# Retention and two MoE layers on one core: the next block's x split behind the second tile's transposes, one mean subtraction on VectorE, S1's parts ahead of two copies

## The chip, the core and the metric

The kernel runs on one core of a Trainium2 chip. The core has TensorE (matmuls and transposes, PE in the rows), VectorE (DVE), ScalarE (ACT), GpSimd (POOL) and SyncE (SP, which here issues most DMA transfers). Each engine runs its own queue in order; semaphores tie the queues together. The metric is the device time of one execution in microseconds (us), less is better. The time of a kernel is the median over its runs.

## The reference

Retention over 768 positions (4 sequences, 8 heads of 64), then a gated layer and then a second layer with a softmax-like unit and a layer norm, on 3072 tokens of 512. Everything is float32:

```python
state = gamma[None, :, None, None] * state + np.einsum('bhd,bhe->bhde', k[:, :, t], v[:, :, t])
y[:, :, t] = scale * np.einsum('bhd,bhde->bhe', q[:, :, t], state)
...
xn = x / rms * rms_g
silu = g * (1.0 / (1.0 + np.exp(-g)))          # g = xn @ w_gate, val = xn @ w_val
x2 = silu * val @ w_out                        # d_ff 1536
...
h = x2 @ w_in                                  # 1024 wide
sm = e / (np.sum(e, axis=-1, keepdims=True) + 1e-09)   # e = exp(h - max)
solu = h * sm
ln = (solu - mu) / np.sqrt(var + 1e-06) * g_ln
return (ln @ w_out).astype(np.float32)
```

## The kernel before

**Blocks.** The tokens are worked in six blocks of 512 (n = 0 to 5), and each block has two stages. The first (gate, value and out, in 12 chunks) makes x2 in the four banks X0 to X3 of PSUM (`XB`). The second, the D stage, makes h, its unit and the result in tiles t = 0 to 3 of 128 tokens. While block n runs, retention for a later block, its x (`xT`) and the next block's first products are worked in the gaps of the same queues. Every product of two float32 matrices is three matmuls on fp32r values: each operand is split in a high part and a low part, and the products high x high, high x low and low x high are summed. `split` (lines 99 to 102) makes the two parts of a tile: a cast on ScalarE gives the high part (line 100), and a subtraction gives the low part (line 101) on VectorE or, where it says so, on GpSimd.

**The D stage of blocks 2 to 5** is `de_quarters` (line 1090). It forms h with seven products of quarters instead of eight (`p1` to `p7`; matmuls on line 1141), whose operands include sums S1 to S4 of quarters of x2. S1 is split on VectorE, S3 and S4 on GpSimd, S2 inline (lines 1116 and 1117). `keep` copies a bank with ScalarE (line 1151) and `add` adds a bank to what is kept with VectorE (line 1155). Then four steps are made for each tile, in this order: soft(2), soft(0), t_tr(2), soft(3), soft(1), t_tr(0), e_mm(2), t_tr(3), e_mm(0), t_tr(1), e_mm(3), e_mm(1). Tile 2 is therefore the first and tile 0 the second.

- `soft` (line 983) computes exp, the products h x e with their sums (line 997), the mean (lines 999 and 1000) and subtracts the mean (line 1002): the first half of 512 columns on VectorE, the second on GpSimd.
- `t_tr` (line 1007) transposes the tile, four transposes of 128 columns for each of two banks (line 1013), casts each bank to its high part (line 1016, ScalarE) and takes the low part (line 1017, VectorE). A square (line 1020) and small operations (lines 1022 to 1028) give the factor of the layer norm.
- `e_mm` (line 1031) is the last product, 24 matmuls (lines 771 to 773), the scaling of its bank (line 1053) and the store (line 1054).

**The next x.** In blocks 2 and 3 the x of the next block is split in four pieces by `xn_split_t`, low parts on GpSimd. Block 5 is the one whose gate and value products use the seven-product form too (`SEVEN`), so block 4 runs `x_sums` (line 425) instead: three splits of plain pieces, four differences (line 437) and four splits of sums into tiles tagged rq, rk, kd and qd. All low parts and differences are GpSimd's. Their matmuls are those of line 883.

**What sets the order.** The program is written as steps hung on numbered slots: `extra[(n, s)]` holds what is emitted when the slot s of block n comes. The slots of the next x stand in the tuple `r` of the block loop. A scheduler then orders the instructions of each engine when the program is built. `tc.issue_after(i)` is a constraint on that order: what is issued under it is placed behind i. It is no semaphore and no wait on the chip. `recent["hi"]` names the instruction behind which the splits of the next x are placed.

Of the kernel before, what the change touches and what calls it, by code (L numbers as in the profile page):

```python
# [9 lines left out]
F32 = mybir.dt.float32  # L10
# [5 lines left out]
ALU = mybir.AluOpType  # L16
# [26 lines left out]
def retention_moe_kernel(ctx: ExitStack, tc: tile.TileContext, qk0, q2, kt, kv, wpk, w2i, w2o,  # L43
# [936 lines left out]
    def halves(t):  # L980
        return t[:, 0, :], t[:, 1, :]

    def soft(n, t, H, e, u, final):
        V = nc.vector
        sm = wt("sm", [P, 12], F32, 4)
        mx, se, su = sm[:, 0:2], sm[:, 2:4], sm[:, 4:6]
        nmx, mu = sm[:, 6:7], sm[:, 7:8]
        for hf in range(2):
            V.tensor_reduce(out=mx[:, hf:hf + 1], in_=H[hf], axis=AX.X, op=ALU.max)
        V.tensor_reduce(out=nmx, in_=mx, axis=AX.X, op=ALU.max, negate=True)  # L990
        for hf in range(2):
            nc.scalar.activation(e[hf], H[hf], AF.Exp, bias=nmx, accum_out=se[:, hf:hf + 1])
        if final and n not in (1, NB - 1) and PRE & 1:

            nc.scalar.activation(sm[:, 11:12], se[:, 1:2], AF.Silu)
        for hf in range(2):
            V.scalar_tensor_tensor(out=u[:, hf, :], in0=H[hf], scalar=1.0, in1=e[hf],
                                   op0=ALU.mult, op1=ALU.mult, accum_out=su[:, hf:hf + 1])
        V.tensor_tensor(out=mu, in0=su[:, 0:1], in1=su[:, 1:2], op=ALU.add)
        V.tensor_scalar(mu, mu, 1.0 / D_FF2, None, ALU.mult)  # L1000
        for hf, eng in ((0, V), (1, nc.gpsimd)):
            i = eng.tensor_scalar(u[:, hf, :], u[:, hf, :], mu, None, ALU.subtract)
            if eng is V:
                recent["sub"] = i
        lnst[t] = (u, sm)

    def t_tr(t, banks=None):
# [3 lines left out]
        for b in range(2):  # L1011
            bank = (banks or HB[t])[b]
            recent["t"] = run([lambda j=j: nc.tensor.transpose(bank[:, j * P:j * P + P], u[:, b, j * P:j * P + P], ident)  # L1013
                 for j in range(4)])
            hi, lo = r2(), r2()
            nc.scalar.copy(hi, bank)
            recent["lo"] = nc.vector.tensor_tensor(out=lo, in0=bank, in1=hi.bitcast(F32), op=ALU.subtract)
            res.append((hi, lo))
# [71 lines left out]
    def de_quarters(n, base):  # L1090
# [26 lines left out]
        s2l = V.tensor_tensor(out=S2[1], in0=s2, in1=S2[0].bitcast(F32), op=ALU.subtract)  # L1117
        S3 = parts(s3, nc.gpsimd)
        with tc.issue_after(i.ins):
            for k in range(2):  # L1120
                V.tensor_tensor(out=s1[:, k, :], in0=XB[2 + k][:, hi], in1=s1[:, k, :], op=ALU.add)
        S1 = parts(s1, V)
        s4 = two(st())
# [67 lines left out]
        p1(0, GB)  # L1191
        with tc.issue_after(s2h.ins):
            p1(1, VB)
        with tc.issue_after(s2l.ins):
            p2(0, X0)
# [5 lines left out]
        p4(0, GB)  # L1201
        soft(n, 2, (GB, u[2][:, 1, :]), halves(e2()), u[2], False)
        p3(0, X1)
# [14 lines left out]
        with tc.issue_after(recent["sub"].ins):  # L1218
            soft(n, 1, (u[1][:, 0, :], u[1][:, 1, :]), halves(e2()), u[1], True)
        t_tr(0, (X0, X1))  # L1220
        e_mm(n, 2, base + 15, GB)
        t_tr(3, (X0, X1))
# [137 lines left out]
    for n in range(NB):  # L1360
        if n + 1 < NB:
# [4 lines left out]
            else:  # L1366
                begin, span, r = 0, 28, (30, 31, 32, 32, 33, 33, 46, 47, 48, 49)
                extra.setdefault((n, 31), []).append(lambda n=n: t_load(0, n))
# [7 lines left out]
            if n + 1 in SEVEN:  # L1376
                r = (30, 31, 32, 32, 33, 33, 46, 46, 47, 47, 48, 48, 49, 49, 50, 51, 52)
                first7 = [lambda: seven_load(n + 1)] \
# [96 lines left out]
```

## Time and profile before

| | before |
|---|---|
| median of 3 runs | 992.1 us (989.67 to 993.05) |
| the profiled execution | 989.03 us, span 987.2 us |
| granted TensorE clock, mean | 0.993 of full |
| TensorE busy | 966.5 us (98% of the span) |
| VectorE, ScalarE, GpSimd busy | 511.7, 422.0, 455.3 us |
| chain of waits that ended last | TensorE 85%, VectorE 5%, GpSimd 3% |

The rows come from the profiled execution alone; its time includes what lies around the span. Busy time tells which engine could set the time. The waits of a queue tell where that engine stood still, and which instruction ended the wait. The timelines tell what the releasing engine did before.

The D stages of blocks 2 to 5 lie, in us of the span, at about 479 to 528, 638 to 690, 796 to 850 and 937 to 985.

### The profile page before, as it was taken

Reading aid. Unit: us, or ns where it says so; the run is one execution under the profiler, and the core shown is the slowest. Engines: PE = TensorE matmul, PEld = TensorE weight load, DVE = VectorE, ACT = ScalarE, POOL = GpSimd, SP = SyncE. Lnnn points to the kernel's source line nnn. Section 1 sums busy time; section 2 is a strip of 40 time slices with the busy share of each in tenths; the row PEclk is TensorE's granted clock in tenths of the full one; section 3 lists DMA queues with packets and bytes.
Section 4 is the critical chain, followed back from the end, with each engine's and each line's share of the span. In section 5 each row is a group of like instructions: output and inputs, shape, how many; then the busy total and the mean of one; then the engine's idle time right before and its main releaser. Section 6 shows DMA issues by size and latency. Waiting matters only on the chain.

```text
span 987.2 us, 16094 instructions
## 1 busy us (share of the span) xinstructions
PE 966.5 (98%) x5868; PEld 803.6 (81%) x5868; DVE 511.7 (52%) x992; ACT 422.0 (43%) x824; POOL 455.3 (46%) x537
## 2 busy tenths in 40 slices
PE   8999999999999999999999999999999999999998
PEld 7878787888888888888878888877888877999977
DVE  5788784652464744333584223576323367444473
ACT  4767664582353444222554222355312346321344
POOL 6976873771143594353364324567042438000032
PEclk9799999999999999999999999999999999999999
DMA  9699999987512116888723889934599954698501
GB/s 350 243 328 407 351 317 379 330 295 235 168 54 87 50 58 226 306 302 267 243 96 128 301 304 327 318 105 133 162 335 310 319 181 148 212 315 295 193 1 44
DMA packets 94991, 227.65 MB, mean 231 GB/s; under 512 B 10816, under 2 KB 36800, under 8 KB 93888
## 3 DMA queue, kind: packets, MB, share of 16 engines
q1 hardware_dynamic: 86128, 201.44, 60.0%
q10 hardware_dynamic: 8784, 25.17, 6.6%
q8 instruction: 47, 0.77, 0.3%
q14 instruction: 32, 0.26, 0.1%
HBM read 184.63 MB, written 41.94 MB: 230 GB/s over the span
## 4 chain that ended last, share of the span: by engine, by line
PE 85%; DVE 5%; POOL 3%; DMA 2%; ACT 2%; issue 1%; SPq 0%; ACTq 0%; POOLq 0%; DVEq 0%
PE X L771 11%; PE X L772 10%; PE X L773 10%; PE GB L773 6%; PE GB L771 6%; PE GB L772 6%; PE VB L771 6%; PE VB L772 5%; PE VB L773 5%; PE SB L119 3%; PE YB L119 2%; PE VB L883 2%; PE YB L883 2%; PE GB L1141 2%; PE X L1141 2%; PE X L1013 2%
## 5 line engine op out<-in xcount | busy, mean ns | idle before, releaser
L790 DVE TENSOR_TENSOR f<-VB,f 128x512 f32<-128x512 f32 x60 | 41.4, 689 | 152.9 <-PE VB L773 121.1
L772 PE MATMUL X<-r,wo 128*128 128x512 f32 x260 | 101.9, 392 | 0.0
L773 PE MATMUL X<-r,wo 128*128 128x512 f32 x260 | 101.4, 390 | 0.0
L819 ACT ACTIVATE f<-GB 128x512 f32<-128x512 f32 x60 | 35.7, 595 | 150.3 <-PE GB L773 147.9
L771 PE MATMUL X<-r,wo 128*128 128x512 f32 x260 | 99.7, 394 | 0.0
L100 ACT CAST r<-f 128x512 fp32r<-128x512 f32 x72 | 44.6, 619 | 118.2 <-DVE f L790 99.8
L672 POOL TENSOR_TENSOR st<-st,x 128x512 int32<-128x512 int32 x52 | 70.5, 1358 | 46.3 <-DVE st L671 12.0
L771 PE MATMUL GB<-xnh,w 128*128 128x512 f32 (+1 forms) x220 | 86.0, 391 | 1.0 <-ACT xnh L100 0.7
L772 PE MATMUL GB<-xnl,w 128*128 128x512 f32 (+1 forms) x220 | 85.6, 389 | 0.3 <-DVE xnl L101 0.2
L771 PE MATMUL VB<-xnh,w 128*128 128x512 f32 (+1 forms) x220 | 85.6, 389 | 0.0
L773 PE MATMUL VB<-xnh,w 128*128 128x512 f32 (+1 forms) x220 | 85.3, 388 | 0.3 <-POOL w L101 0.3
L773 PE MATMUL GB<-xnh,w 128*128 128x512 f32 (+1 forms) x220 | 85.5, 388 | 0.1
L772 PE MATMUL VB<-xnl,w 128*128 128x512 f32 (+1 forms) x220 | 85.1, 387 | 0.0
L567 POOL TENSOR_TENSOR x<-x 128x512 f32<-128x512 f32 x24 | 31.9, 1331 | 95.4 <-DMA x<-scr 43.0
L101 DVE TENSOR_TENSOR r<-f,r 128x512 fp32r<-128x512 f32 x72 | 59.4, 826 | 30.9 <-ACT r L100 30.2
L101 POOL TENSOR_TENSOR r<-st,r 128x512 fp32r<-128x512 f32 x8 | 10.9, 1368 | 112.4 <-ACT r L100 110.8
L773 PEld LDWEIGHTS X<-r,wo 128*128 128x128 f32 x260 | 48.8, 188 | 10.2
L771 PEld LDWEIGHTS X<-r,wo 128*128 128x128 f32 x260 | 48.8, 188 | 10.2 <-ACT r L100 0.2
L772 PEld LDWEIGHTS X<-r,wo 128*128 128x128 f32 x260 | 48.8, 188 | 10.0 <-issue 0.2
L771 PE MATMUL X<-w2oh,r 128*128 128x512 f32 (+1 forms) x144 | 56.4, 391 | 0.0
L773 PE MATMUL X<-w2oh,r 128*128 128x512 f32 (+1 forms) x144 | 56.3, 391 | 0.0
L772 PE MATMUL X<-w2ol,r 128*128 128x512 f32 (+1 forms) x144 | 55.4, 385 | 0.0
(451 smaller groups left out, 2485.6 us busy)
## 6 DMA issues: line engine op xcount, KB each, us to landing
w<-scr SPq DMA_DIRECT2D x96, 512.0 KB, 4.9
wo<-scr SPq DMA_DIRECT2D x59, 512.0 KB, 5.4
x<-in_wpk SPq DMA_DIRECT2D x36, 512.0 KB, 6.3
x<-scr SPq DMA_DIRECT2D x25, 512.0 KB, 6.2
sscr<-x SPq DMA_DIRECT2D x24, 512.0 KB, 7.7
scr<-CV ACTq DMA_DIRECT2D x18, 512.0 KB, 5.9
rv<-in_kv SPq DMA_DIRECT2D x24, 256.0 KB, 4.6
scr<-w ACTq DMA_DIRECT2D x12, 512.0 KB, 6.0
```

What stands on the lines that cost most here:

```text
L100: h = nc.scalar.copy(hi, src)
L101: (lo_eng or nc.vector).tensor_tensor(out=lo, in0=src, in1=hi.bitcast(F32), op=ALU.subtract)
L119: return lambda: nc.tensor.matmul(out, lhsT=lhsT, rhs=rhs, start=start, stop=stop)
L567: nc.gpsimd.tensor_tensor(out=w[:, 0, :], in0=w[:, 0, :], in1=w[:, 1, :], op=ALU.add)
L672: nc.gpsimd.tensor_tensor(out=ti, in0=ti, in1=lo, op=ALU.add)
L771: nc.tensor.matmul(ps, lhsT=lh, rhs=rh, start=start, stop=False)
L772: nc.tensor.matmul(ps, lhsT=lh, rhs=rl, start=False, stop=False)
L773: return nc.tensor.matmul(ps, lhsT=ll, rhs=rh, start=False, stop=stop)
L790: recent["dve"] = nc.vector.tensor_tensor(out=a, in0=GV[1], in1=silu[:, 0, :], op=ALU.mult)
L819: recent["act"] = nc.scalar.activation(s[:, 0, :], GV[0], AF.Silu)
L883: nc.tensor.matmul(ps, lhsT=x, rhs=y[:, k, :], start=start and k + i == 0, stop=k == 1 and i == 2, skip_group_check=True)
L1141: last["mm"] = nc.tensor.matmul(bank, lhsT=x[:, k, ts_], rhs=y[:, k, :], start=start and k + i == 0, stop=k == 1 and i == 2, skip_group_ch ...
```

## The change

It has three parts. In `soft` the engine of the second half's mean subtraction becomes an argument, and the first tile (t = 2) passes VectorE. `t_tr` notes its last high cast, and behind t_tr(0) the constraint for the splits of the next x is set to it; their slots move from 46 to 49 (46 to 52 in block 4) to 50 and 51 (50 to 53). In `de_quarters` S1's cast and low part are written out and placed ahead of S3's split, and `p1(1)` with its copy and `p2` come behind them in order.

```diff
@@ -980,7 +980,7 @@
     def halves(t):
         return t[:, 0, :], t[:, 1, :]
 
-    def soft(n, t, H, e, u, final):
+    def soft(n, t, H, e, u, final, other=nc.gpsimd):
         V = nc.vector
         sm = wt("sm", [P, 12], F32, 4)
         mx, se, su = sm[:, 0:2], sm[:, 2:4], sm[:, 4:6]
@@ -998,7 +998,7 @@
                                    op0=ALU.mult, op1=ALU.mult, accum_out=su[:, hf:hf + 1])
         V.tensor_tensor(out=mu, in0=su[:, 0:1], in1=su[:, 1:2], op=ALU.add)
         V.tensor_scalar(mu, mu, 1.0 / D_FF2, None, ALU.mult)
-        for hf, eng in ((0, V), (1, nc.gpsimd)):
+        for hf, eng in ((0, V), (1, other)):
             i = eng.tensor_scalar(u[:, hf, :], u[:, hf, :], mu, None, ALU.subtract)
             if eng is V:
                 recent["sub"] = i
@@ -1013,7 +1013,7 @@
             recent["t"] = run([lambda j=j: nc.tensor.transpose(bank[:, j * P:j * P + P], u[:, b, j * P:j * P + P], ident)
                  for j in range(4)])
             hi, lo = r2(), r2()
-            nc.scalar.copy(hi, bank)
+            recent["thi"] = nc.scalar.copy(hi, bank)
             recent["lo"] = nc.vector.tensor_tensor(out=lo, in0=bank, in1=hi.bitcast(F32), op=ALU.subtract)
             res.append((hi, lo))
         se, r, vs, w = sm[:, 2:4], sm[:, 8:9], sm[:, 9:10], sm[:, 10:11]
@@ -1115,11 +1115,15 @@
         S2 = two(r2()), two(r2())
         s2h = S.copy(S2[0], s2)
         s2l = V.tensor_tensor(out=S2[1], in0=s2, in1=S2[0].bitcast(F32), op=ALU.subtract)
-        S3 = parts(s3, nc.gpsimd)
         with tc.issue_after(i.ins):
             for k in range(2):
                 V.tensor_tensor(out=s1[:, k, :], in0=XB[2 + k][:, hi], in1=s1[:, k, :], op=ALU.add)
-        S1 = parts(s1, V)
+        S3 = two(r2()), two(r2())
+        S1 = two(r2()), two(r2())
+        s1h = S.copy(S1[0], s1)
+        s1l = V.tensor_tensor(out=S1[1], in0=s1, in1=S1[0].bitcast(F32), op=ALU.subtract)
+        with tc.issue_after(s1h.ins):
+            split(*S3, s3, nc.gpsimd)
         s4 = two(st())
         for k in range(2):
             V.tensor_tensor(out=s4[:, k, :], in0=XB[2 + k][:, lo], in1=s2[:, k, :], op=ALU.subtract)
@@ -1189,9 +1193,9 @@
             mul(W, t, S4, B22), add(u[t][:, 1, :], W, u[t][:, 1, :]), step()
 
         p1(0, GB)
-        with tc.issue_after(s2h.ins):
+        with tc.issue_after(s2h.ins), tc.issue_after(s1h.ins):
             p1(1, VB)
-        with tc.issue_after(s2l.ins):
+        with tc.issue_after(s2l.ins), tc.issue_after(s1l.ins):
             p2(0, X0)
         p6(0, GB)
         p5(0, X1)
@@ -1199,7 +1203,7 @@
         c22(0, X1)
         p6(1, VB)
         p4(0, GB)
-        soft(n, 2, (GB, u[2][:, 1, :]), halves(e2()), u[2], False)
+        soft(n, 2, (GB, u[2][:, 1, :]), halves(e2()), u[2], False, V)
         p3(0, X1)
         p7(1, VB, e2())
         p5(1, X3)
@@ -1218,6 +1222,7 @@
         with tc.issue_after(recent["sub"].ins):
             soft(n, 1, (u[1][:, 0, :], u[1][:, 1, :]), halves(e2()), u[1], True)
         t_tr(0, (X0, X1))
+        recent["hi"] = recent["thi"]
         e_mm(n, 2, base + 15, GB)
         t_tr(3, (X0, X1))
         e_mm(n, 0, base + 17, X2)
@@ -1364,7 +1369,7 @@
             elif n == 1:
                 begin, span, r = 35, 21, (57, 58, 59, 59, 60, 60, 61, 62, 63, 64)
             else:
-                begin, span, r = 0, 28, (30, 31, 32, 32, 33, 33, 46, 47, 48, 49)
+                begin, span, r = 0, 28, (30, 31, 32, 32, 33, 33, 50, 50, 51, 51)
                 extra.setdefault((n, 31), []).append(lambda n=n: t_load(0, n))
                 if n + 1 not in SEVEN:
                     for s, i, part in ((39, 0, 0), (39, 0, 1), (47, 1, 0), (48, 1, 1)):
@@ -1374,7 +1379,7 @@
             for i, f in enumerate(pieces):
                 extra.setdefault((n, begin + i * span // (len(pieces) - 1)), []).append(f)
             if n + 1 in SEVEN:
-                r = (30, 31, 32, 32, 33, 33, 46, 46, 47, 47, 48, 48, 49, 49, 50, 51, 52)
+                r = (30, 31, 32, 32, 33, 33, 50, 50, 50, 51, 51, 51, 51, 52, 52, 53, 53)
                 first7 = [lambda: seven_load(n + 1)] \
                     + [lambda i=i: w_load((n + 1) * NM + i, 2) for i in range(2)] + [seven_pump]
                 for s, f in zip((47, 48, 48, 51), first7):
```

What the build makes of it is shown at three places. The rows are those of the engines' order, without times; X_68 to X_71 are the banks X0 to X3, f_572 is the tile of t = 2, f_568 of t = 0, x_575 of t = 3, and lines from 1122 on stand four or five lower in the changed file.

GpSimd in the D stage of block 2, before (xnl is the low part of the next x, `L1002` the mean subtraction, L1024 to L1028 small operations):

```order
L236 TENSOR_TENSOR kd_5199<-rv_5077,ktab_t 128x512
L101 TENSOR_TENSOR xnl<-xT,xnh 128x512 x4
L1024 TENSOR_TENSOR sm_4628<-sm_4628 128x1
L1002 TENSOR_SCALAR f_572_4605<-f_572_4605,sm_4628 128x512
L322 TENSOR_TENSOR xT<-xT,rg_t 128x4x128
L1024 TENSOR_TENSOR sm_4666<-sm_4666 128x1
L1002 TENSOR_SCALAR f_568_4571<-f_568_4571,sm_4666 128x512
```

and in the changed kernel:

```order
L1024 TENSOR_TENSOR sm_4664<-sm_4664 128x1
L1002 TENSOR_SCALAR f_568_4571<-f_568_4571,sm_4664 128x512
L1026 TENSOR_SCALAR sm_4628<-sm_4628 128x1
L1027 TENSOR_TENSOR sm_4628<-sm_4628,mhalf 128x1
L1028 TENSOR_TENSOR sm_4628<-sm_4628 128x1
L1024 TENSOR_TENSOR sm_4718<-sm_4718 128x1
L1002 TENSOR_SCALAR x_575_4647<-x_575_4647,sm_4718 128x512
L1025 TENSOR_TENSOR sm_4664<-sm_4664 128x1
L101 TENSOR_TENSOR xnl<-xT,xnh 128x512 x2
L1026 TENSOR_SCALAR sm_4664<-sm_4664 128x1
L101 TENSOR_TENSOR xnl<-xT,xnh 128x512 x2
```

The four low parts stand behind the subtractions of tiles 0 and 3, and tile 2's subtraction is gone from this engine.

VectorE in the same stage, from the first tile's mean to the second tile's products (L997), before:

```order
L1000 TENSOR_SCALAR sm_4628<-sm_4628 128x1
L1002 TENSOR_SCALAR f_572_4605<-f_572_4605,sm_4628 128x512
L1155 TENSOR_TENSOR x_575_4647<-X_71,x_575_4647 128x512
L989 TENSOR_REDUCE sm_4666<-f_568_4571 128x1 x2
L1155 TENSOR_TENSOR f_569_4579<-X_70,f_569_4579 128x512
L990 TENSOR_REDUCE sm_4666<-sm_4666 128x1
L997 SCALAR_TENSOR_TENSOR f_568_4571,sm_4666<-f_568_4571,st_4664 128x512
L997 SCALAR_TENSOR_TENSOR f_568_4571,sm_4666<-f_568_4571,st_4665 128x512
L1022 TENSOR_SCALAR sm_4666<-sm_4666 128x1
L1017 TENSOR_TENSOR r_581_4694<-X_68,r_580_4693 128x512
```

and in the changed kernel (L1159 is L1155 of before):

```order
L1000 TENSOR_SCALAR sm_4628<-sm_4628 128x1
L1002 TENSOR_SCALAR f_572_4605<-f_572_4605,sm_4628 128x512 x2
L1159 TENSOR_TENSOR x_575_4647<-X_71,x_575_4647 128x512
L989 TENSOR_REDUCE sm_4664<-f_568_4571 128x1 x2
L1159 TENSOR_TENSOR f_569_4579<-X_70,f_569_4579 128x512
L990 TENSOR_REDUCE sm_4664<-sm_4664 128x1
L1017 TENSOR_TENSOR r_581_4690<-X_68,r_580_4689 128x512
L997 SCALAR_TENSOR_TENSOR f_568_4571,sm_4664<-f_568_4571,st_4662 128x512
L997 SCALAR_TENSOR_TENSOR f_568_4571,sm_4664<-f_568_4571,st_4663 128x512
```

Two subtractions stand in a row, and the low part of X_68 (L1017) moves ahead of the two products.

TensorE in block 5, from the end of tile 0's last product (X_70) to the first of tile 3's (X_71), with tile 3's transposes (x_1101), before:

```order
L771 MATMUL X_70<-w2oh,r_1115_8962 128x512
L772 MATMUL X_70<-w2ol,r_1115_8962 128x512
L1013 MATMUL X_68<-ident,x_1101_8851 128x128 x4
L1013 MATMUL X_69<-ident,x_1101_8851 128x128 x4
L773 MATMUL X_70<-w2oh,r_1116_8963 128x512
L771 MATMUL X_70<-w2oh,r_1115_8962 128x512
```

and in the changed kernel:

```order
L772 MATMUL X_70<-w2ol,r_1115_8962 128x512
L773 MATMUL X_70<-w2oh,r_1116_8963 128x512
L1013 MATMUL X_68<-ident,x_1101_8851 128x128 x4
L1013 MATMUL X_69<-ident,x_1101_8851 128x128 x4
L771 MATMUL X_71<-w2oh,r_1118_9005 128x512
```

ScalarE at that place, where L1016 of X_68 is the cast of tile 3's first bank and L1053 the scaling of tile 0's result, before:

```order
L992 ACTIVATE x_1111_8937,sm_8938<-f_1097_8787,sm_8938 128x512 x2
L1016 CAST r_1118_9005<-X_68 128x512
L1020 ACTIVATE x_1101_8851,sm_8918<-x_1101_8851 128x1024
L1016 CAST r_1120_9013<-X_69 128x512
L1053 ACTIVATE f_1122_9049<-X_70,sm_8868 128x512
```

and in the changed kernel:

```order
L992 ACTIVATE x_1111_8937,sm_8938<-f_1097_8787,sm_8938 128x512 x2
L1053 ACTIVATE f_1122_9049<-X_70,sm_8868 128x512
L1016 CAST r_1118_9005<-X_68 128x512
L1020 ACTIVATE x_1101_8851,sm_8918<-x_1101_8851 128x1024
L1054 DMA out<-f_1122_9049 128x512
```

The transposes move from inside tile 0's product to its end, and the scaling moves ahead of the cast.

## Rows read from the trace of the kernel before

**Rows 1.** Part 1 of the page: busy us (share) xinstructions of each engine.

```profile
PE 966.5 (98%) x5868; PEld 803.6 (81%) x5868; DVE 511.7 (52%) x992; ACT 422.0 (43%) x824; POOL 455.3 (46%) x537
```

**Rows 2.** Waits of TensorE's queue: engine, line, releaser, us in total, times, longest.

```profile
PE X L1013 <- POOL f L1002: 4.8, 3, 2.1
PE GB L773 <- DVE r L1017: 2.0, 2, 1.7
...
PE X L1141 <- DVE r L101: 1.1, 2, 0.5
...
PE SB L119 <- DVE A L262: 0.9, 1, 0.9
...
PE GB L771 <- ACT xnh L100: 0.7, 1, 0.7
```

**Rows 3.** Timeline of TensorE, block 2: start us, us, engine, line, operation [idle before <-releaser].

```profile
501.79 0.65 PE L1013 MATMUL X<-ident,f 128*128 128x128 f32 x4 [2.13 <-POOL f L1002]
502.20 0.47 PE L1141 MATMUL X<-w2ih,r 128*128 128x512 f32 x1
...
506.38 0.39 PE L773 MATMUL GB<-w2oh,r 128*128 128x512 f32 x1
506.61 0.39 PE L771 MATMUL GB<-w2oh,r 128*128 128x512 f32 x1
```

**Rows 4.** Timeline of GpSimd, block 2, ahead of the same transposes.

```profile
494.37 5.67 POOL L101 TENSOR_TENSOR xnl<-xT,xnh 128x512 fp32r<-128x512 f32 x4 [1.62 <-PE VB L1141]
...
500.17 1.57 POOL L1002 TENSOR_SCALAR f<-f,sm 128x512 f32<-128x512 f32 x1
```

**Rows 5.** Timeline of VectorE, block 2: the first tile's second product and subtraction.

```profile
495.03 1.18 DVE L997 SCALAR_TENSOR_TENSOR f<-f,x 128x512 f32<-128x512 f32 x1
...
497.61 1.29 DVE L1002 TENSOR_SCALAR f<-f,sm 128x512 f32<-128x512 f32 x1
```

**Rows 6.** Timeline of VectorE, block 5: the same two instructions.

```profile
951.91 0.69 DVE L997 SCALAR_TENSOR_TENSOR f<-f,x 128x512 f32<-128x512 f32 x1
...
953.02 0.49 DVE L1002 TENSOR_SCALAR f<-f,sm 128x512 f32<-128x512 f32 x1
```

**Rows 7.** Timeline of TensorE, block 5: the first tile's eight transposes.

```profile
955.94 1.04 PE L1013 MATMUL X<-ident,f 128*128 128x128 f32 x8
```

**Rows 8.** Windows behind the two stops: us, TensorE busy (x), granted clock, DMA share, GB/s.

```profile
502.70:506.10 3.40, 3.40 (x9) 0.51 0.00 0
...
661.00:665.00 4.00, 3.87 (x19) 1.00 0.00 0
```

**Rows 9.** Timelines of VectorE and TensorE, block 4: a low part and its wait.

```profile
818.56 1.76 DVE L997 SCALAR_TENSOR_TENSOR f<-f,st 128x512 f32<-128x512 f32 x1
...
821.11 0.49 PE L773 MATMUL GB<-w2oh,r 128*128 128x512 f32 x1 [1.71 <-DVE r L1017]
```

**Rows 10.** Timeline of VectorE, block 4: S1's low part and the addition ahead.

```profile
800.38 0.69 DVE L1155 TENSOR_TENSOR f<-X,f 128x512 f32<-128x512 f32 x1
801.29 1.37 DVE L101 TENSOR_TENSOR r<-st,r 128x512 fp32r<-128x512 f32 x1 [0.22 <-ACT r L100]
```

**Rows 11.** Timeline of ScalarE, block 5: tile 3's first cast, tile 0's scaling.

```profile
969.55 0.56 ACT L1016 CAST r<-X 128x512 fp32r<-128x512 f32 x1
...
971.84 0.69 ACT L1053 ACTIVATE f<-X,sm 128x512 f32<-128x512 f32 x1 [0.20 <-PE X L773]
```

**Rows 12.** Timeline of GpSimd, block 4: splits, differences and sums of the next x.

```profile
810.62 4.50 POOL L101 TENSOR_TENSOR xnl<-xT,xnh 128x512 fp32r<-128x512 f32 x3 [5.28 <-PE VB L1141]
...
816.79 2.98 POOL L437 TENSOR_TENSOR xT<-xT 128x512 f32<-128x512 f32 x2
...
833.22 1.29 POOL L101 TENSOR_TENSOR qd<-xT,qd 128x512 fp32r<-128x512 f32 x1
```

**Rows 13.** Timelines of TensorE and GpSimd, block 5: tile 0's transposes, tile 3's subtraction.

```profile
964.76 0.60 PE L1013 MATMUL X<-ident,f 128*128 128x128 f32 x4
...
965.96 1.72 POOL L1002 TENSOR_SCALAR x<-x,sm 128x512 f32<-128x512 f32 x1
```

## The prediction

> **What bounds the kernel now.** I read the busy table of the page first: TensorE is busy for 966.5 of 987.2 us [rows 1]. The other engines are far below, so their work costs time only where TensorE stops for it. Next I read the waits of TensorE's queue [rows 2]: the changed code can touch five of its lines, 4.8 + 2.0 + 1.1 + 0.9 + 0.7 us. Last I read the timelines around those stops.
>
> The largest, 4.8 us in three blocks, is the first tile's transposes (t=2) waiting for the mean subtraction on GpSimd. In block 2 the second four transposes start at 501.79 after 2.13 us of waiting [rows 3]. GpSimd ran the four low parts of the next x from 494.37 to 500.04 and the 1.57 us subtraction only behind them, from 500.17 to 501.74 [rows 4]. VectorE had finished its own half by 498.90, though it was slow as well: beside GpSimd's work the second product (L997) took 1.18 us and the subtraction 1.29 us [rows 5]. Block 5 is the control. It has no next x, the same two instructions take 0.69 and 0.49 us [rows 6], and all eight transposes follow each other from 955.94 without a wait [rows 7].
>
> The stop in block 2 has a second price. Behind it the granted clock was 0.51 of full for 3.40 us [rows 8], which is nearly all at the lower level, 1.2 GHz; later matmuls start 0.23 us apart again, 506.38 and 506.61 [rows 3]. That stretch lost 0.49 x 3.40 = 1.7 us. In block 3 the longest wait was the same 2.1 us and the clock stayed at 1.00 [rows 8]: whether a stop is followed by the lower clock is not fixed by its length alone.
>
> **The change part by part.**
>
> *(a) Order and engine of the first tile.* GpSimd's four low parts now stand behind tile 0's and tile 3's subtractions; tile 2's subtraction is gone from GpSimd, and VectorE does two in a row. The cost on VectorE is one more instruction of 0.49 us [rows 6] in each of four blocks. With no low part ahead of it the chain is block 5's: 0.69 and 0.49 us instead of 1.18 and 1.29. In blocks 2 and 3 it then ends 0.49 + 0.80 - 0.49 = 0.8 us before VectorE's half alone ended so far, and the transposes follow without a stop: -4.8 us. The L1155 addition behind it keeps its time in blocks 2 and 3 and comes 0.5 us later in block 5; the bank that it reads is not needed again at once, so I count nothing; without that cover it is 0.5 us. With the stop the low clock goes: -1.7 us (bounds -1.7 and 0, since it may come behind another stop).
>
> *(b) The first low part of tile 2.* VectorE's L1017 now stands ahead of tile 0's two products. TensorE waited for it in two blocks, 1.71 us of the 2.0 [rows 2] in block 4, where the product ahead of it was stretched to 1.76 us [rows 9] while GpSimd formed the x sums. Both reasons go: -2.0 us. Late next is the second low part, which still stands behind tile 0's subtraction; no row shows TensorE waiting for it, even in block 4.
>
> *(c) S1's parts.* TensorE waited 0.5 us each in two blocks [rows 2] for S1's low part, which started at 801.29 behind an L1155 of 0.69 us and a short wait for its cast [rows 10]. Ahead of that addition it is ready at least 0.5 us earlier: -1.1 us. The addition moves by up to the low part's 1.37 us and the copy of VB on ScalarE by one cast; the banks that they free are written again only after other products. I take 0, bounds 0 and 0.7 in each of four blocks.
>
> *(d) Attention.* Its matmuls, masks (L262) and loads now fall behind tiles 3 and 1, mostly into the next block's gate stage. The 0.9 us wait for a mask product [rows 2] falls in the D stage and goes: -0.9. At the new place the masks stand between the gate stage's products, where VectorE is idle most of the time. On SP's queue attention's loads move behind two w4 loads, and their matmuls move back further than that. I take 0, bounds 0 and 0.9 for one round in each of two blocks.
>
> Removed: 4.8 + 1.7 + 2.0 + 1.1 + 0.9 = 10.5 us.
>
> *(e) What is new.* In block 5 tile 3's eight transposes move from inside tile 0's product to behind it, straight ahead of tile 3's product, and ScalarE's scaling of tile 0's result (L1053, 0.69 us) stands ahead of the first cast of the transposed tile (0.56 us) [rows 11]. TensorE must wait for that cast: 0.69 + 0.56, less the 0.4 us of the second four transposes (502.20 - 501.79 in [rows 3]), is 0.85, and with some latency I take 1.0 us (bounds 0.2, where the scaling costs nothing, and 1.3). In blocks 2 to 4 matmuls of the next block stand in that gap. In block 4 the x sums on GpSimd end later: taken 0.5, bounds 0 and the first rival's 6.2. About ten more switches between fp32 transposes or attention and fp32r products, each under 0.1 us by the same two rows, give 0.5 (bounds 0 and 1). The next block's first products can wait for a later high or low part: 0.7 us was paid once [rows 2]; I take 0.2, bounds 0 and 0.7. Together 2.2 us.
>
> GpSimd's low parts now run beside VectorE's chain of tile 1, and such company made 1.29 us of 0.49 [rows 5, 6]. I take 0 for it: in block 4 the x sums already ran beside the chains of tiles 3 and 1, and the three waits of L1013 in [rows 2] are all tile 2's. The Trainium skill has a rule that speaks against this part ("SBUF — State Buffer", section "Who interferes with whom"): VectorE and GpSimd share one port pair as an exclusive lock, taken by a VectorE instruction with two SBUF inputs or in a two-port mode, and whoever starts second is blocked. [Rows 5] against [rows 6] agree, and by the rule alone tile 1 would be held up as tile 2 was, with the time of the second rival.
>
> Sum: 2.2 - 10.5 = -8.3 us. The profiled execution took 989.03 us for a span of 987.2, so it would take 980.7. It lies 3.1 us below the median of the runs, 992.1, and runs of one kernel vary by that much; against the median I forecast 992.1 - 8.3 = **983.8 us**.
>
> **The rivals.**
>
> *First rival: the sums come too late (about the same time).* In block 4 GpSimd splits three pieces of the next x, takes four differences and splits four sums. Before, this ran from 810.62 to 834.51, 23.9 us [rows 12]. Now it can start only behind tile 0's second cast. From tile 0's second transposes to the first product that reads a low part of a sum, TensorE has 62 products of 0.23 us, 16 short ones of the next block at about half of that and 16 transposes (4 x 0.4 us), 17.7 us together. If the chain needed its 23.9 us up to there, TensorE would wait 6.2, and 7.9 with the lower clock behind it. In place of the 0.5 that is -8.3 + 7.4 = -0.9: 991.2 us. For it: each sum waits for the one before. Against it: the 23.9 us hold waits, three subtractions and the last sums. By block 5's rows tile 3's subtraction, which stands ahead, ends 967.68 - 964.76 = 2.9 us after those transposes [rows 13]; behind it come three parts (4.50 us), five of 1.3 to 1.5 [rows 12], a subtraction and small ones, some 13.5 us. That is 16.4 of 17.7 us: just in time, which is why I took 0.5 and not 0. Chance 0.10.
>
> *Second rival: the collision moves to tile 1 (slower).* In blocks 2 to 4 the low parts (5.67 us [rows 4]) now run beside VectorE's chain of tile 1. They start 2.9 us behind tile 0's second transposes; with another tensor operation of 1.4 and tile 1's own subtraction of 1.57 GpSimd is through at 11.5, and TensorE reaches tile 1's transposes after 48 products, ten or more others and eight transposes, at 13 us or later. From 1.5 us of delay on, TensorE stops again. If VectorE's chain is held up as in [rows 5], 0.49 + 0.80 and as much in its small operations, every block pays the 2.1 us of [rows 2] at tile 1, and if the clock falls each time, 1.7 more: 3 x 3.8 = 11.4 us, and the forecast's -8.3 becomes +3.1: 995.2 us. Against it: block 4 before, as under (e). Chance 0.06.
>
> That the change would not do what it says is excluded for (a) to (c): the engines' order shows each move.
>
> **How the numbers follow.** What a measurement can tell from no change is 0.3%, 3 us: faster is below 989.1, slower above 995.1. The forecast holds with 0.82; 0.02 is left for small mishaps that no row shows. Faster: 0.82. Same: 0.12, the first rival and the mishaps. Slower: 0.06, the second rival. The range: if the new costs are 0.2 instead of 2.2, 981.8, less 2 us for runs that fall low, 980. On the other side, without the 1.7 and the 0.9 and with 1.3, 2, 1 and 0.7 for the new costs, 5.0 - 7.9 = -2.9, 989. So 980 to 989; both rivals lie outside, and with the mishaps they are 0.18.
>
> **What would show it.** Right: no wait of L1013 for GpSimd; for tile 2 two L1002 on VectorE of about 0.45 us each and L997 at 0.69; GpSimd's low parts of x behind tile 0's transposes; the clock at 1.00 in the D stage of block 2; no L773 waiting for L1017 and no wait for S1; one new wait of about 1 us in block 5, L771 for ScalarE's L1016. Wrong: TensorE waiting for xnh, xnl or a part of the sums (kd, rk, rq, qd) around the end of a D stage (first rival), for L1002 of tiles 3 or 1 (second rival), or a stretch at 1.2 GHz behind any new stop.

## The result and the profile after

| | before | changed |
|---|---|---|
| median of 4 runs each | 991.1 us | 980.7 us (979.1 to 982.3) |
| ratio, 95% interval | | 0.9894 (0.9868 to 0.9920) |
| the profiled execution | 989.03 us, span 987.2 | 982.31 us, span 980.4 |
| TensorE busy | 966.5 us (98%) | 966.5 us (99%) |
| TensorE's share of the chain that ended last | 85% | 90% |

The kernel is 10.4 us faster, where 8.3 was forecast; 980.7 us lies in the range of 980 to 989, close to its low end. The point forecast of 983.8 us is 3.1 us too high: 1.0 of it is the kernel before, whose median was 992.1 us over three runs and is 991.1 over four, and 2.1 is the change. Measured twice more on other occasions, with up to six runs, the ratio was 0.9893 (0.9873 to 0.9914) and 0.9897 (0.9880 to 0.9915).

The two profiles differ by only 6.8 us in span, because the profiled execution of the changed kernel lost time at its start, which the change does not reach. So I measure the changed part by itself: from the first product of block 2's D stage to the end of the span. Here are the two starts, on TensorE's timeline, before:

```profile
479.05 0.39 PE L1141 MATMUL GB<-w2ih,x 128*128 128x512 f32 x1
```

and changed:

```profile
482.54 0.39 PE L1145 MATMUL GB<-w2ih,x 128*128 128x512 f32 x1
```

Before, the part took 987.2 - 479.05 = 508.15 us, now 980.4 - 482.54 = 497.86: 10.3 us less, as in the medians. Two later profiles of the changed kernel gave 497.90 and 497.92. This measure repeats far better than the whole time, whose first 170 us vary by some us between executions; the experiments use it beside the ratio. Of the kernel before there is one profile, so its 508.15 us is a single reading.

The waits of TensorE's queue in the changed kernel answer to [rows 2]:

```profile
PE X L771 <- ACT f L1053: 0.6, 1, 0.6
...
PE GB L771 <- ACT xnh L100: 0.6, 1, 0.6
...
PE X L771 <- ACT r L1016: 0.5, 1, 0.5
PE GB L883 <- DVE st L896: 0.3, 1, 0.3
```

No L1013 waits for GpSimd or VectorE, no L773 for L1017, no D-stage product for S1, no L119 for a mask. The wait for xnh in the second row stands at 161 us, ahead of everything that the change reaches. Three waits are new: the cast in block 5, as forecast, and two that were not, the scaling of tile 0's result (X2) in block 4 and 0.3 us for a VectorE operation (L896) at the start of block 5.

TensorE's timeline at the first tile's transposes in blocks 2 and 3, against [rows 3]:

```profile
502.55 1.03 PE L1013 MATMUL X<-ident,f 128*128 128x128 f32 x8
...
657.71 1.03 PE L1013 MATMUL X<-ident,f 128*128 128x128 f32 x8
658.50 0.48 PE L1145 MATMUL X<-w2ih,r 128*128 128x512 f32 x1
```

All eight transposes stand in a row, and the product behind them starts 658.50 - 657.71 = 0.79 us after the first. In block 2, a window around the place shows the granted clock at 1.00 (the value behind the count of matmuls), against 0.51 in [rows 8]:

```profile
502.00:511.00 9.00, 9.00 (x49) 1.00 0.37 141
```

VectorE, first tile (against [rows 5]) and last tile of block 2:

```profile
498.52 0.69 DVE L997 SCALAR_TENSOR_TENSOR f<-f,x 128x512 f32<-128x512 f32 x1
...
499.63 0.88 DVE L1002 TENSOR_SCALAR f<-f,sm 128x512 f32<-128x512 f32 x2
...
516.48 1.18 DVE L997 SCALAR_TENSOR_TENSOR f<-f,x 128x512 f32<-128x512 f32 x1 [1.26 <-ACT x L992]
...
518.92 0.52 DVE L999 TENSOR_TENSOR sm<-sm 128x1 f32<-128x1 f32 x1
...
519.67 1.29 DVE L1002 TENSOR_SCALAR f<-f,sm 128x512 f32<-128x512 f32 x1
```

and GpSimd from tile 3's subtraction on:

```profile
512.87 1.58 POOL L1002 TENSOR_SCALAR x<-x,sm 128x512 f32<-128x512 f32 x1
...
514.56 2.55 POOL L101 TENSOR_TENSOR xnl<-xT,xnh 128x512 fp32r<-128x512 f32 x2
...
517.78 2.90 POOL L101 TENSOR_TENSOR xnl<-xT,xnh 128x512 fp32r<-128x512 f32 x2
...
522.78 1.58 POOL L1002 TENSOR_SCALAR f<-f,sm 128x512 f32<-128x512 f32 x1
```

Tile 2's second product takes 0.69 us, and its two subtractions 0.88 together. The low parts of x start at 514.56, right behind tile 3's subtraction. And the collision is not gone: tile 1's product, a small operation and its subtraction are stretched to 1.18, 0.52 and 1.29 us, as tile 2's product and subtraction were in [rows 5]. It has only moved to a chain that TensorE does not wait for. GpSimd ends tile 1's half at 524.36, and in order it is needed at the second four of tile 1's transposes:

```profile
524.38 0.60 PE L1013 MATMUL X<-ident,f 128*128 128x128 f32 x4
...
528.95 0.60 PE L1013 MATMUL X<-ident,f 128*128 128x128 f32 x4
```

That is 4.6 us to spare in block 2. In block 3 it is 4.6 us too, in block 4 1.8.

### The profile page after: what moved, and what is told of

It is laid out like the page before. It is cut to its first block, busy times and chain, and to the rows that moved or that the text cites. A ratio compares the mean times of both kernels' runs of the same rounds, so it can differ in the third digit from the quotient of the medians.

```text
span 980.4 us, 16072 instructions
## 1 busy us (share of the span) xinstructions
PE 966.5 (99%) x5868; PEld 805.4 (82%) x5868; DVE 504.6 (51%) x996; ACT 422.9 (43%) x824; POOL 447.1 (46%) x533
## 4 chain that ended last, share of the span: by engine, by line
PE 90%; POOL 3%; DMA 2%; DVE 2%; ACT 2%; issue 1%; SPq 0%; ACTq 0%; POOLq 0%; DVEq 0%
PE X L771 11%; PE X L773 10%; PE X L772 10%; PE GB L771 7%; PE GB L773 7%; PE GB L772 6%; PE VB L771 6%; PE VB L773 6%; PE VB L772 6%; PE SB L119 3%; PE X L1145 3%; PE GB L1145 2%; PE VB L1145 2%; PE YB L119 2%; PE VB L883 2%; PE YB L883 2%
## 5 line engine op out<-in xcount | busy, mean ns | idle before, releaser
L773 PE MATMUL X<-r,wo 128*128 128x512 f32 x260 | 101.4, 390 | 0.0
L773 PE MATMUL VB<-xnh,w 128*128 128x512 f32 (+1 forms) x220 | 85.6, 389 | 0.0
L773 PE MATMUL GB<-xnh,w 128*128 128x512 f32 (+1 forms) x220 | 85.4, 388 | 0.0
L101 DVE TENSOR_TENSOR r<-f,r 128x512 fp32r<-128x512 f32 x72 | 61.7, 858 | 32.6 <-ACT r L100 32.1
L773 PEld LDWEIGHTS X<-r,wo 128*128 128x128 f32 x260 | 48.8, 188 | 10.2
L773 PE MATMUL X<-w2oh,r 128*128 128x512 f32 (+1 forms) x144 | 55.6, 386 | 0.0
```

The costliest lines, as they stand in the source:

```text
L101: (lo_eng or nc.vector).tensor_tensor(out=lo, in0=src, in1=hi.bitcast(F32), op=ALU.subtract)
L773: return nc.tensor.matmul(ps, lhsT=ll, rhs=rh, start=False, stop=stop)
```

## The experiments

All ratios are against the kernel before, measured beside it on the same chip, with their 95% interval. "Part" is the time from the first product of block 2's D stage to the end of the span.

| kernel | ratio (interval) | part, us | against before |
|---|---|---|---|
| before | | 508.15 | |
| changed, three profiles | 0.9893 (0.9873 to 0.9914) | 497.86, 497.90, 497.92 | -10.3 |
| engine alone | 0.9984 (0.9969 to 0.9998) | 985.8 - 479.99 = 505.81 | -2.3 |
| order alone | 0.9924 (0.9911 to 0.9936) | 979.7 - 479.02 = 500.68 | -7.5 |
| S1 alone | 0.9985 (0.9974 to 0.9996) | 985.5 - 478.88 = 506.62 | -1.5 |
| order and S1 | 0.9914 (0.9901 to 0.9928) | 980.1 - 481.11 = 498.99 | -9.2 |
| splits one tile earlier | 0.9886 (0.9864 to 0.9908) | 978.2 - 479.38 = 498.82 | -9.3 |
| splits one tile later | 0.9952 (0.9934 to 0.9971) | 982.4 - 479.87 = 502.53 | -5.6 |
| transposes inside, all blocks | 0.9899 (0.9874 to 0.9923) | 984.3 - 485.70 = 498.60 | -9.6 |
| transposes inside, block 5 | 0.9887 (0.9869 to 0.9905) | 975.4 - 478.52 = 496.88 | -11.3 |
| transposes inside, blocks 4 and 5 | 0.9880 (0.9862 to 0.9898) | 976.1 - 479.53 = 496.57 | -11.6 |

**The engine alone.** The kernel before with this edit (`soft` also gets the argument `other`, GpSimd where nothing is passed):

```diff
-        for hf, eng in ((0, V), (1, nc.gpsimd)):
+        for hf, eng in ((0, V), (1, other)):
...
-        soft(n, 2, (GB, u[2][:, 1, :]), halves(e2()), u[2], False)
+        soft(n, 2, (GB, u[2][:, 1, :]), halves(e2()), u[2], False, V)
```

> Only the engine of the first tile's second mean subtraction is changed; the splits and sums of the next x stay where they were, and S1 too. Theory (the order did it; the engine alone helps, but only where the order is left as it was): VectorE's two subtractions run beside GpSimd's low parts at about 1.3 us each, so in blocks 2 and 3 they end near 500.2 of the old time axis, 0.8 us behind the end of the first four transposes (499.06 + 0.36). The wait of L1013 falls from 4.8 to 1 to 2 us, now released by VectorE, and the low clock behind it may go; the 2.0 us of L1017 and the 1.1 us of S1 stay. 3 to 5.5 us faster than before, ratio 0.9945 to 0.997. Rival (the engine did it): all that the whole change gave, 8 us or more, ratio 0.992 or less.

Its waits:

```profile
PE X L1013 <- DVE f L1002: 2.1, 4, 0.7
PE SB L119 <- DVE A L262: 1.8, 2, 0.9
...
PE GB L883 <- DVE st L896: 1.3, 1, 1.3
...
PE X L771 <- ACT r L1016: 0.5, 1, 0.5
```

L1013's wait fell to 2.1 us, 0.7 in blocks 2 and 3, as expected and by VectorE. So most of the old 2.1 us stop, 1.4 us, came from standing behind the low parts in GpSimd's queue; what is left are VectorE's two subtractions beside GpSimd. The low clock behind the stop went too. L1017's waits went and S1's fell from 1.1 to 0.7 us, though I had expected both to stay. Yet the gain was only 1.6 us by the ratio and 2.3 by the part, under both expectations: other places took time back. L119 now waits for a mask in both blocks 2 and 3, an L883 waits 1.3 us, and block 5 has its cast's wait already; about 1 us more stands in gaps too short for the list of waits and is not assigned. The cast's wait matters: it belongs to the engine's part of the change, not to the order's.

**The order alone.**

```diff
-            nc.scalar.copy(hi, bank)
+            recent["thi"] = nc.scalar.copy(hi, bank)
...
         t_tr(0, (X0, X1))
+        recent["hi"] = recent["thi"]
-                begin, span, r = 0, 28, (30, 31, 32, 32, 33, 33, 46, 47, 48, 49)
+                begin, span, r = 0, 28, (30, 31, 32, 32, 33, 33, 50, 50, 51, 51)
...
```

> Only the place of the next x's splits and sums is changed (slots and the cast that they stand behind); GpSimd still subtracts the second half of the first tile, and S1 is as before. Theory (the order did it): GpSimd has nothing ahead of that subtraction and ends it, as in block 5 of the kernel before (953.17 + 1.77 = 954.94, transposes from 955.94), ahead of need. No wait of L1013 over 0.3 us, no low clock, L1017's 2.0 us gone; S1's waits of 1.1 us stay. 8 to 9.5 us faster, ratio 0.9905 to 0.992. Rival (the engine did it): at least 3 us of L1013's wait stay and the gain is under 5 us, ratio above 0.995.

```profile
499.03 1.03 PE L1013 MATMUL X<-ident,f 128*128 128x128 f32 x8
```

The eight transposes of block 2 stand in a row although GpSimd still subtracts the second half; so they do in blocks 3 to 5. What stayed are S1's two waits and small ones for L1017:

```profile
PE X L1141 <- DVE r L101: 1.1, 2, 0.5
...
PE GB L773 <- DVE r L1017: 1.0, 4, 0.3
```

The gain is 7.5 us both by ratio and by part, a little under the 8 to 9.5 that I had expected, and far from the rival's 5. That the order removes L1013's waits is shown; the waits for L1017, 0.25 us in each block, I had not expected to stay.

**S1 alone.**

```diff
-        S1 = parts(s1, V)
+        s1h = S.copy(S1[0], s1)
+        s1l = V.tensor_tensor(out=S1[1], in0=s1, in1=S1[0].bitcast(F32), op=ALU.subtract)
...
+        with tc.issue_after(s2l.ins), tc.issue_after(s1l.ins):
             p2(0, X0)
```

> Only S1's parts are moved ahead of the copy and the addition. Theory: the two waits of 0.54 us for S1's low part go and nothing else: L1013 keeps 4.8 us for GpSimd, L1017 2.0 us, the lower clock may stand behind one or another of the stops. About 1.1 us faster, ratio 0.9975 to 1.0005. Rival (S1's earlier place also lets the first tile's chain start earlier): L1013's wait grows or shrinks by over 0.5 us and the gain is above 2.5 us or below zero.

```profile
PE X L1013 <- POOL f L1002: 4.7, 3, 2.1
PE GB L773 <- DVE r L1017: 2.0, 2, 1.7
```

S1's waits are gone, and those for the first tile and for L1017 are as they were. Not as expected, the mask's 0.9 us went as well, and in block 2 tile 3's transposes wait 0.4 us for GpSimd's subtraction. The part is 1.5 us shorter. From the first product of its D stage to that of the next, or to the end, block 4 takes 140.5 us instead of 141.3 and block 5 49.0 instead of 49.8: 0.8 us in each of the two blocks where S1's waits of 0.54 stood. Blocks 2 and 3 together are the same within 0.1. This run also shows the clock. Both stops of 2.13 us stand where they stood, but now the clock falls behind the one in block 3 (0.56 from 661 to 664.5) and not behind the one in block 2:

```profile
498.00:506.00 8.00, 5.75 (x29) 1.00 0.26 105
661.00:664.50 3.50, 3.50 (x11) 0.56 0.00 0
```

**Order and S1, without the engine.**

> The whole change without the engine: splits and sums behind the second tile's transposes, S1's parts ahead, and the first tile's second half subtracted by GpSimd. Theory (with the order right the engine is worth nothing): the same as the whole change, 9 to 11 us faster than before, ratio 0.9885 to 0.991, no wait of L1013 over 0.3 us. Rival (the engine is needed as well): 3 us or more of the gain are missing, ratio 0.9925 or more, with waits of L1013 for GpSimd in each block.

The waits of L1013 are gone, as in the order alone, and the ratio is between theory and rival: 1.1 us of the part are missing against the changed kernel. One reason is read in the timeline of block 2:

```profile
504.33 0.50 PE L773 MATMUL GB<-w2oh,r 128*128 128x512 f32 x1 [0.27 <-DVE r L1017]
```

VectorE has its L1017 behind tile 0's products here, and TensorE waits for it in each block, as in the order alone. With the engine changed as well, the scheduler puts L1017 ahead of them (the second place shown of the engines' order). But the changed kernel also has its three new waits, and this version has none of them. So the engine is worth 1.1 us net. By blocks, from D stage to D stage, the changed kernel is 0.66 and 0.67 us shorter in blocks 2 and 3 and 0.05 in block 4, and 0.30 longer in block 5, where the cast's wait stands. L1017's stop accounts for 0.42 us of the 0.66 (504.33 - 503.68 - 0.23, with the product ahead starting at 503.68); the rest is not assigned. For the first tile's transposes themselves the subtraction on VectorE is not needed.

**The splits one tile earlier**, behind tile 2's transposes, with slots 48 to 51:

```diff
         t_tr(2, (X0, X1))
+        recent["hi"] = recent["thi"]
...
         t_tr(0, (X0, X1))
-        recent["hi"] = recent["thi"]
...
```

> The changed kernel with the next x's splits and sums placed one tile earlier, behind tile 2's transposes instead of tile 0's; GpSimd's low parts then stand right behind tile 0's subtraction and ahead of tile 3's. Theory (what counts is only whether the low parts stand ahead of a subtraction that TensorE needs soon, and run beside its VectorE chain): tile 2 has no wait, but tile 3's subtraction, or tile 3's chain on VectorE, is late, and TensorE waits 0.5 to 2 us for it in blocks 2 to 4; 1 to 5 us slower than the changed kernel, ratio 0.991 to 0.995. Rival (any place behind tile 2's transposes does): the same as the changed kernel within 1 us.

```profile
PE X L771 <- ACT r L1016: 1.9, 2, 1.5
```

The rival is right for the time: it is the changed kernel's within the interval, 0.9 us behind by the part. No transpose waits for a subtraction. In block 4 the product behind tile 3's transposes stops 1.5 us for their cast, in place of the changed kernel's 0.6 and 0.3, and in block 3 a product of the D stage waits 0.5 us for a low part of GpSimd's.

**The splits one tile later**, behind tile 3's transposes, with slots 52 to 55:

```diff
-        recent["hi"] = recent["thi"]
         e_mm(n, 2, base + 15, GB)
         t_tr(3, (X0, X1))
+        recent["hi"] = recent["thi"]
...
```

> The changed kernel with the next x's splits and sums placed one tile later, behind tile 3's transposes. By my count the sums of block 4 had 1.3 us to spare (16.4 of 17.7 us) in the changed kernel. Theory (the lateness of the x parts is the second bound of the place): the chain starts some 5 us later, and TensorE waits for parts of the x or of the sums around the end of the D stage, 2 to 5 us in block 4 and 0 to 2 us in each of blocks 2 and 3; 2 to 8 us slower than the changed kernel, ratio 0.992 to 0.998. Rival (TensorE's queue has other products to fill the gap): within 1 us of the changed kernel.

```profile
PE X L771 <- ACT r L1016: 1.8, 4, 0.5
...
PE X L773 <- DVE r L1017: 0.7, 2, 0.4
PE GB L883 <- ACT rq L100: 0.6, 1, 0.6
PE VB L883 <- POOL rk L101: 0.6, 1, 0.6
```

4.6 us slower than the changed kernel by the part, as the theory said, but only a third of it for the theory's reason: parts of the sums, rq and rk, come 0.6 us late each in block 4. Most of the rest is block 5's wait for the cast, which now stands in blocks 2 to 4 too, with a wait for a low part behind it in two of them: without the next x no product of the next block can stand between tile 3's transposes and its product. The place of the splits has a bound on either side, and the side that is late costs more.

**Transposes inside the product.** First in all blocks (`mid=recent["t"]` without a condition), then in block 5 alone, then in blocks 4 and 5, which is the edit shown:

```diff
+            with tc.issue_after(mid.ins) if mid is not None and f == 5 else nullcontext():
                 mm3(bank, hi[:, cs], lo[:, cs], w2["oh"][:, f, :], w2["ol"][:, f, :], f == 0, f == NF - 1)
...
-        e_mm(n, 0, base + 17, X2)
+        e_mm(n, 0, base + 17, X2, mid=recent["t"] if n >= 4 else None)
         t_tr(1, (X0, X1))
-        e_mm(n, 3, base + 19, X3)
+        e_mm(n, 3, base + 19, X3, mid=recent["t"] if n == 5 else None)
```

> The changed kernel, with the last nine products of tile 0 and of tile 3 placed behind the next tile's transposes, so that these stand inside a product and the casts run beside it. Theory (the new waits of the changed kernel are the casts and scalings behind transposes that stand at a product's end): the 0.46 us in block 5 and the 0.59 us in block 4 go, and no other comes; 0.5 to 1.2 us faster than the changed kernel, ratio 0.988 to 0.9895 against before. Rival (the transposes then come too early for the subtraction of tile 3 or 1): waits of L1013 for L1002 of 0.5 us or more, and no gain or a loss against the changed kernel.

The two new waits went, but others came, and by the time it is the changed kernel: neither the theory's gain nor the rival's wait of 0.5 us is there.

```profile
PE GB L771 <- ACT f L819: 1.0, 2, 0.5
...
PE GB L1146 <- DMA xnh<-t2scr: 0.6, 1, 0.6
...
PE X L1013 <- POOL f L1002: 0.3, 1, 0.3
```

By stages the last one, from tile 2's transposes of block 5 to the end, fell from 980.4 - 948.77 = 31.6 to 984.3 - 953.64 = 30.7 us, while blocks 2 to 4 grew. Hence the next two. (The load of xnh that came late in block 4 is in no other profile; why is open.)

> The changed kernel with tile 3's and tile 1's transposes placed inside the product before them in block 5 alone, where no product of a next block can fill the gap. Theory (the new wait of block 5 comes from transposes at a product's end with nothing behind them): the 0.46 us wait for the cast goes and the last stage, from tile 2's transposes of block 5 to the end, falls from 31.6 by 0.5 to 1.0 us; blocks 2 to 4 stay within 0.2 us of the changed kernel. Against before the ratio is 0.988 to 0.9905; the time alone will hardly tell it from the changed kernel. Rival (the wait only moves to a later cast or to the subtraction of tile 1): the last stage stays within 0.2 us of 31.6.

> As the version with block 5 alone, and in block 4 tile 3's transposes also stand inside tile 0's product. Theory (block 4's 0.59 us wait for tile 0's scaling is set by ScalarE's queue, where the cast of a sum waits for GpSimd ahead of it, and not by the transposes' place): block 4 stays within 0.3 us of the changed kernel, block 5 gains as in the other version. Rival (the transposes' place sets it): the wait for L1053 in block 4 goes and block 4 is 0.5 us shorter.

> The changed kernel once more, for comparison on the same chip. From the first product of block 2's D stage to the end of the span it took 497.9 us in both profiles so far; all theories: 497.7 to 498.1 again, ratio against before 0.988 to 0.991.

Block 5 alone gained 1.0 us by the part, as expected. With block 4 as well it is 1.35, and there the rival was right: the wait for tile 0's scaling is in no row any more, and block 4 is 0.35 us shorter. Blocks 2 and 3 take 155.17 and 154.73 us, from D stage to D stage, in both versions and in the changed kernel, so these small differences can be read. Block 5's transposes of tiles 2, 3 and 1 in the version with both, on TensorE's timeline:

```profile
945.44 1.03 PE L1013 MATMUL X<-ident,f 128*128 128x128 f32 x8
...
957.50 1.03 PE L1013 MATMUL X<-ident,x 128*128 128x128 f32 x8
...
963.87 1.03 PE L1013 MATMUL X<-ident,f 128*128 128x128 f32 x8
```

The last stage is 976.1 - 945.44 = 30.7 us. At 977.9 us in the median, ratio 0.9880 (0.9862 to 0.9898), it is the fastest of all, but only the part tells it from the changed kernel; the intervals of the whole time overlap.

## Why the prediction was right, and where its sizes were off

*Term (a), first tile: right in kind, short in size.* I counted 4.8 us of waits and 1.7 of low clock, and both are gone. But a stop costs more than its row of waits says, since the row counts from the end of the matmul ahead: a product lasts 0.39 us in the timeline, and without a stop the next one starts 0.23 us after it ([rows 3]), so that each stop also takes the 0.16 us by which they would have overlapped. In block 3 before, from the first four transposes to the product behind the second four:

```profile
657.91 0.60 PE L1013 MATMUL X<-ident,f 128*128 128x128 f32 x4
...
661.04 0.47 PE L1141 MATMUL X<-w2ih,r 128*128 128x512 f32 x1
```

That is 661.04 - 657.91 = 3.13 us, where the changed kernel needs 0.79 (above): 2.34 us for a wait given as 2.12. The same holds for the others: S1's operand cost 802.71 - 801.56 - 2 x 0.23 = 0.69 for 0.54, L1017's in block 4 821.11 - 819.00 - 0.23 = 1.88 for 1.71. Eight stops, with 0.15 to 0.22 us each beside the row, and one of 0.3 us in block 3 that no row of waits lists, make some 1.6 us. This is the step that failed: the sum took the column of waits, 8.8 us, as the price, and the stops measure some 10.4.

*Term (a), which part did it.* The forecast gave the gain to both halves of (a) together. The runs split it: the order alone takes all of L1013's waits and the clock with them; the engine adds 1.1 us net, the gain from L1017's place less the new waits.

*Terms (b), (c), (d): right.* L1017's 2.0, S1's 1.1 and attention's 0.9 us are gone. S1 alone gave 1.5 us by the part. The additions and copies that were moved cost nothing that can be read. Term (b) is shared: the order takes the 1.71 us stop, but with the order alone 0.25 us stayed in each block, and only with the engine does the scheduler move L1017.

*Term (e), block 5: right place, half the size.* 0.46 us of wait, against 1.0 (bounds 0.2 and 1.3):

```profile
962.90 1.03 PE L1013 MATMUL X<-ident,x 128*128 128x128 f32 x8
964.40 0.50 PE L771 MATMUL X<-w2oh,r 128*128 128x512 f32 x1 [0.46 <-ACT r L1016]
...
963.18 0.69 ACT L1053 ACTIVATE f<-X,sm 128x512 f32<-128x512 f32 x1
963.77 0.58 ACT L1016 CAST r<-X 128x512 fp32r<-128x512 f32 x1
```

Start to start it is 964.40 - 962.90 - 0.79 = 0.71 us, and the version with the transposes inside gained 1.0. ScalarE's scaling began at 963.18, 0.28 us after the first transpose, and the cast at 963.77, right behind it; I had let the scaling start only when the first four transposes were done. Where a cast waits for its transposes alone it starts 0.63 us after the first of them, as in block 2 behind the transposes at 524.38 (above):

```profile
525.01 0.59 ACT L1016 CAST r<-X 128x512 fp32r<-128x512 f32 x1 [1.88 <-PE X L1013]
```

So the scaling held the cast of block 5 up by only 963.77 - 962.90 - 0.63 = 0.24 us.

*Term (e), the sums: nothing, and a stop of the same size elsewhere.* I took 0.5 us for TensorE waiting for a sum's part. No product waits for one. Instead tile 1's product, which is made in X2, waits 0.59 us until tile 0's result has been scaled out of that bank; that the sizes are alike is luck. ScalarE, GpSimd and TensorE at that place in block 4:

```profile
831.96 0.62 ACT L100 CAST rk<-xT 128x512 fp32r<-128x512 f32 x1 [2.94 <-POOL xT L437]
832.67 0.59 ACT L1016 CAST r<-X 128x512 fp32r<-128x512 f32 x1
833.15 0.69 ACT L1053 ACTIVATE f<-X,sm 128x512 f32<-128x512 f32 x1
...
831.89 0.20 POOL L1028 TENSOR_TENSOR sm<-sm 128x1 f32<-128x1 f32 x1
...
832.03 1.03 PE L1013 MATMUL X<-ident,f 128*128 128x128 f32 x8
...
833.90 0.50 PE L771 MATMUL X<-w2oh,r 128*128 128x512 f32 x1 [0.59 <-ACT f L1053]
```

The cast of rk waited 2.94 us on ScalarE for a difference of GpSimd's, and the scaling stood behind it in the queue. It looks as if the late sums reached TensorE that way, and so I expected it of the version with blocks 4 and 5; but there the wait went when only the transposes' place was changed. The rows agree with that run: the cast of rk was over at 832.58, and tile 1's first cast (832.67) came 0.64 us after tile 1's transposes began (832.03), no later than the cast of block 2 that waited for its transposes alone (0.63). What held the scaling up is that it stands behind this cast in ScalarE's order. The sums do have a part in how early it could have come at all: GpSimd, between its differences, made tile 0's factor (L1028), which the scaling needs, only by 832.09. What ScalarE's order and that factor would each cost alone is not shown. The margin I had counted as 1.3 us for the first low part of a sum was 1.2: GpSimd ends it at 836.23, and the products that read it start at 837.44. That it fits is in part luck: from tile 0's second transposes (818.35) on both ends came 1.4 to 1.5 us later than counted, 17.9 us for 16.4 and 19.1 for 17.7.

```profile
834.93 1.30 POOL L101 TENSOR_TENSOR rk<-xT,rk 128x512 fp32r<-128x512 f32 x1
...
837.44 0.76 PE L883 MATMUL VB<-rk,w 128*128 128x256 f32 x5
```

*The first rival* fell by that margin, and the run with the splits one tile later shows that it was real: one tile on, TensorE waits for rq and rk.

*The second rival* had its mechanism right and its price wrong. Tile 1's chain is stretched just as tile 2's was, in block 2 by up to 0.80 us an instruction (1.29 against 0.49). The Trainium skill ("SBUF — State Buffer", section "Who interferes with whom") says that VectorE and GpSimd contend for a shared port pair when a VectorE instruction has two SBUF inputs or is in a two-port mode. The trace agrees: tile 1's product and subtraction, which began while a low part ran, took 1.18 and 1.29 us, and the product at 517.59, which began 0.2 us ahead of a low part (517.78), kept its 0.68. But the second four of tile 1's transposes come 4.6 us after GpSimd's subtraction in block 2, and no row shows TensorE waiting. The rule tells which instructions get longer; whether that costs anything is read from the queue that waits for them.

*The net.* Removed were not 10.5 but about 12.1 us, start to start. New are three stops of 0.7, 0.75 and 0.5 us, counted in the same way. The ten more switches between transposes and fp32r products, for which I had taken 0.5 us, are hardly seen: the gaps under 0.12 us between the starts of successive matmuls of the part, beyond 0.2275 us for 512 columns and 0.118 for 256, sum to about 5.8 us before and 6.1 after. New costs are then some 2.2 us, the forecast's total with other members, which is luck. Together -9.9, against -10.3 measured on the part; 0.4 us stays unassigned.

*Open:* why the clock falls behind one of two equal stops (block 2 in the profile before, block 3 in S1 alone). Up to TensorE's last product no other profile has the lower clock in the part, and shorter stops were not followed by it: 1.71 us before, 1.45 with the splits one tile earlier, 1.32 with the engine alone. Whether it fell in every execution before was not shown, so how much of the median's 10.4 us is clock is open too: between nothing and 1.7 us.

## What to carry to other kernels

Where two engines slow each other, move the work that can wait behind the chain that TensorE needs next; the collision itself may stay, if it hits a chain with slack. Count a stop at its start-to-start distance, not at the row of waits, and look at each in-order queue between the late work and TensorE, since the wait may surface behind another instruction. And when a whole time varies at its start, compare profiles from a fixed instruction behind that start to the end.

## What the runs showed that I had not expected

The part from block 2 on repeats within 0.06 us over three profiles of one kernel, while whole executions of it spread from 978.3 to 982.7 us. Moving one subtraction to VectorE changed the scheduler's order elsewhere: tile 3's transposes went to the end of a product in block 5, which costs 0.7 to 1.0 us, and the low part L1017 ahead of two products in each block, which saves 0.4 us a block. Each of these two effects is in all larger than the subtraction's own 0.4 us. And moving the splits a tile earlier, into the neighbourhood that the change left, cost no more than 1 us.
